# Routing steps, pooling adds and weight splits at other turns, and the gate of the expert output on ScalarE

## The chip, the cores and the metric

The kernel runs on one core of one Trainium2 chip. Its five engines work side by side and meet at semaphores: TensorE (PE in the profile; its weight loads are PEld), VectorE (DVE), ScalarE (ACT), GpSimd (POOL) and SyncE (SP), which here only issues DMAs. The metric is the device time of one execution in microseconds (us), lower is better; of several executions the median is taken.

## The reference

Attention over pooled keys, and behind it a mixture of eight experts of which each row uses one:

```python
# q, k, v: 8 batches x 8 heads x 576 rows x 64
k_p = k.reshape(B, H, 72, 8, D).mean(axis=3)      # 8 rows pooled to one
v_p = v.reshape(B, H, 72, 8, D).mean(axis=3)
scores = scale * q @ k_p.T;  attn = softmax(scores)
x = (attn @ v_p)                                   # as 4608 rows x 512
logits = x @ w_gate                                # 4608 x 8
expert = argmax(logits);  gate_w = softmax(logits)[expert]
# a row's position: how many rows before it chose the same expert;
# rows at positions from capacity (N // E * 2 = 1152) on are dropped
h = relu(x_of_expert @ w1[e])                      # 512 -> 1024
y = h @ w2[e]                                      # 1024 -> 512
out[row] = gate_w[row] * y                         # dropped rows: 0
```

All is float32. The inputs q and k are drawn eight times larger than v, so that the softmax is far from flat.

## The kernel before, in words

**Two parts.** The first (to about 216 us) computes attention, decides for each row its expert and its place among that expert's rows, and writes for each slot of each expert which row it holds and with which gate. The second is a loop over tiles of an expert's rows. In both, instructions are issued in program order on each engine (`manual_schedule`): what the text of the kernel emits first on an engine runs first there, and waits there for whatever it needs while all behind it waits too.

**Turns.** The attention works on 36 units of 128 query rows by four heads. Two batches make a pair, a pair has 9 units (`NPU`), and pair p has units 9p to 9p + 8. The loop `for n in range(nu + 2)` (L1028) has 38 turns, n = 0 to 37. "Turn n" below means that iteration. In it unit n is scored (`score`, L479), its maximum taken and subtracted on VectorE (`softmax`; `mx`, `pt`), the next unit's queries transposed (`pq`, L462) and copied by ScalarE to `qT` (L463), and the exponential taken on ScalarE. Unit n - 2 is finished: its weights are transposed (`p_t`, `pp` L502), copied by ScalarE to `pT` (L503), multiplied by the values (`av`, `pa`, L516), and normalised on VectorE (`norm`: `rz` L527, then `xo` and, last, the gate logits `lt` L542). The next unit's `pa` uses the same PSUM tile, so its first product waits for `lt` of the unit before. The value products and the logits share one product: the gate matrix is multiplied into the values beforehand. `n_early` is 25 and `n_start` 33; in `hooks`, `p, j = divmod(n, 9)`.

**Queues written by hand.** Work that is not a unit's own is kept in lists of functions or generators and pulled in small steps at set places of a turn (`step(queue, n)`):

- `rq`, the routings: nearly all on VectorE. One step in `softmax`, the call at L1078 with a number of steps that depends on the turn, and three steps in `norm`. One `route` (L588 on) covers 9 columns of 128 rows: maximum of the logits `gmx`, difference `gd` (L598), the choice `gme` and `gmm`, the one-hot rows `oh` (L614), their sums `su` (L621), a running count, then three empty steps where more than three columns are routed (L631 to L633), count products on TensorE (`po`, L641, 8 to 32 columns wide), position arithmetic (`gps`, `gpos`, `ghi` L662, `gix`), and the gate's reciprocal into `pairs` (L672). Routing 0 enters the queue in turn 10, routing 1 in turn 19, routing 2 in turn 28; three short ones (routing 3) come in turns 32, 35 and 37.
- `sq`, the scatters of `pairs` into `slots` in DRAM (L679, POOL): nine for each routing, two a turn, four a turn from turn 26. `slots` is first filled with a default by a DMA (`setup_rows`, L339), called in `hooks` where n is 12. For routing 1 each scatter has a copy of `mx` to the tile `apart` ahead of it, so that POOL waits for that turn's maximum.
- `gq`, POOL's pooling adds (three adds to a piece of keys or values, `tree`, L370 on) of the pair after next, four a turn; `hooks` puts them in the queue. From turn 26 on the queue holds instead eight pieces of the favourite expert's w1: each is a ScalarE cast `w1h` (L125) and a POOL subtraction `w1l` (L126).
- `dq`, the masks of the capacity (VectorE, turn 27); `hq` and `aq`, preparation of keys, values and loads.

In turns 31 to 34 rows of the favourite expert are gathered and transposed (`pxe`), and in turns 36 and on the first expert tile is begun (`hidden`, `prologue`).

**The loop over tiles** (`For_i`, L1157 on) makes 20 iterations for the input, 15 on two tiles of 128 rows, 5 on one. All float32 products are made as three products of a rounded part and a remainder (`xh`/`xl`, `w1h`/`w1l`, `hh`/`hl`, `w2h`/`w2l`; ScalarE casts, VectorE subtracts). An iteration reads its numbers from a table into registers on each engine (`values_load`), computes h (`hidden_all`, L150: four groups `g` in turn on three PSUM tiles `ph`; ScalarE's relu `hh` L1129 and VectorE's `hl` L1130 empty each), y (`product`, L159) of tile 1 and of tile 0, and between them transposes the next rows (`px`, L1117). Where the next iteration has another expert (`sw`), `split_w1` and `split_w2` cast and subtract the new weights, which SP has loaded one iteration earlier (`load_w1`, `load_w2` into `r1`, `r2`, L118 and L122; a load may start when the splits of the iteration have read them). Both tiles of y are scaled by their rows' gates (`gate`, L1152, on VectorE: `ys`), and POOL scatters them to the output behind a small subtraction that waits for `ys` (`guardf`), after scattering rows of zeros for the dropped ones (`zrow`).

Of the kernel before, what the change touches and what calls it, by code (L numbers as in the profile page):

```python
# [10 lines left out]
F32 = mybir.dt.float32  # L11
# [20 lines left out]
def pooled_attn_top1_moe(ctx: ExitStack, tc: tile.TileContext, q, k, v, wg, w1, w2, cap, out):  # L32
# [129 lines left out]
    with ExitStack() as actx:  # L162
# [421 lines left out]
        def route(bp, t0, G, blk, tail, prods, sc, count=False, run=None):  # L584
# [45 lines left out]
            if gn > 3:  # L630
                yield  # L631
                yield
                yield  # L633
            po = bank([P, 512], "po")[:, 0 : 4 * E].rearrange("p (a e) -> p a e", a=4)
            prods = [x for x in prods if before or x[1] != "c"]
            for n_, (w, x, l, m) in enumerate(prods):
# [102 lines left out]
        with tc.manual_schedule():  # L739
# [265 lines left out]
            def hooks(n):  # L1005

                p, j = divmod(n, NPU)
                if n == 0:
                    red(vps[0][:, NR - 1 :], raws[0][1][2][:, 2:3])
                    pooled(1)  # L1010
                    pool(1)
                if p == B // 2:
                    return
                if p + 2 < B // 2:
                    if j == (4 if p == 0 else 2):
                        load_kv(p + 2)
                    if j == (7 if p == 0 else 5):
                        if p:
                            nc.gpsimd.tensor_copy(apart, early["mx"][:, 0, 0:1])
                        pooled(p + 2)  # L1020
                        pool(p + 2)
                if n == 3 * NB:
                    drain(gq)
                    gq.append(setup_rest())
                    drain(gq)
                    setup_rows()

            for n in range(nu + 2):  # L1028
                u = units[n] if n < nu else None
                p = units[n - 2] if n > 1 else None  # L1030
                nx = units[n + 1] if n + 1 < nu else None
                new = n and u and u.b != units[n - 1].b
                if new:
                    assert not aq
                    ahead(u.b)
                if n == n_start:
                    start_weights()
                if n == n_early:
                    start_early()
                if n == n_early + 1:  # L1040
                    drain(gq)
                    split_early(0, 2 * KD, nc.gpsimd)
                if n == n_early + 3:
                    start_ids()
                if n == n_early + 4:
                    start_rows()
                if u:
                    u.score(0)
                if p:
                    p.p_t(0)  # L1050
                if u:
                    u.score(1)
                    u.softmax()
                step(aq)
                if p:
                    p.p_t(1)
                if n == nu + 1:
                    for c in range(KF):
                        nc.scalar.copy(wr["h"][:, c], wr[2][:, c])
                if n >= nu:  # L1060
                    hidden(0, n - nu)
                if nx:
                    nx.q_part()
                flush()
                step(aq)
                if n == 1:
                    busy(5)
                    hq.append(prep_v(0))
                    step(hq)
                if u:  # L1070
                    u.exp()
                if p:
                    p.open()
                    p.av(0)
                turns(n)
                if p:
                    p.av(1)
                step(rq, 4 if NPU < n < nu - 8 else 8 if n >= nu - 8 else 0)  # L1078
                step(dq)
                if p:  # L1080
                    p.norm()
                    r = route_of(p)
                    if r:
                        rq.append(r)
                        if p.b == early_b - 1:
                            rq.append(favourite())
                hooks(n)
                step(gq, 4 if n <= n_early else 0 if n_early + 3 <= n < n_early + 5 else 2)
                step(sq, 2 if n < nu - 10 else 4)
                step(aq)  # L1090
            flush()
# [4 lines left out]
    with ExitStack() as bctx:  # L1096
# [52 lines left out]
                split(hh[s], hl[s], p)  # L1149

        def gate(i):
            nc.vector.tensor_scalar_mul(ys[i], y[i], io[:, i, 1:2].bitcast(F32))  # L1152

        nc.sync.dma_start(xs[NT : NT + 1, :], zrow[0:1])
        nt = nc.values_load(ntl[0:1, 0:1], min_val=E, max_val=MT // 2 + E)
# [1 line left out]
        with tc.For_i(0, nt, 1, iteration_sync="reg_based") as t:  # L1157
            with tc.manual_schedule():
                two = nc.values_load(cf[0:1, 5, ds(t, 1)], min_val=0, max_val=1)  # L1159
                sw = nc.values_load(cf[0:1, 0, ds(t, 1)], min_val=0, max_val=1)  # L1160
                nw = nc.values_load(cf[0:1, 1, ds(t, 1)], engines=(SP,), min_val=0, max_val=1)
                we = nc.values_load(cf[0:1, 2, ds(t, 1)], engines=(SP,), min_val=0, max_val=E - 1)
                ct = nc.values_load(cf[0:1, 3, ds(t, 1)], engines=(DVE,), min_val=0, max_val=NCOL)  # L1163
                c2 = nc.values_load(cf[0:1, 3, ds(t + 2, 1)], engines=(DVE,), min_val=0, max_val=NCOL)  # L1164
                cd = nc.values_load(cf[0:1, 4, ds(t, 1)], engines=(DVE,), min_val=0, max_val=NCOL)  # L1165
                nc.gpsimd.tensor_sub(io, zi, zi)
                nc.gpsimd.tensor_sub(iz, zi[:, 0], zi[:, 0])
                with tc.If(two > 0) as both:
                    hidden_all()
                    product(y[1], hh, hl, 1)  # L1170
                    transpose_x()
                    product(y[0], hh, hl, 0)
                with both.Else():
                    hidden_one()
                    product(y[0], hh, hl, 0)
                with tc.If(sw > 0):
                    split_w1(0)
                masked(ix[:, :, 0], c2, mkeep)
                gather(xg, ix, xs[:, :])
                split_x()  # L1180
                with tc.If(sw > 0):
                    split_w1(1)
                load_w1(we, cond=nw > 0, bounds_check="skip_entire_dma")
                columns(io[:, :, 1], ids[:, ds(ct, 2), 1])
                masked(io[:, :, 0], ct, mkeep)
                gate(1)
                masked(iz, cd, mdrop)
                nc.gpsimd.tensor_sub(guard[:, 0], iz, iz)
                for i in range(2):
                    scatter(iz[:, i : i + 1], zrow[:, :], across_iterations=True)  # L1190
                gate(0)
                with tc.If(sw > 0):
                    split_w2()
                load_w2(we, cond=nw > 0, bounds_check="skip_entire_dma")
                for i in (1, 0):
                    nc.gpsimd.tensor_sub(guardf, ys[i][:, 0:2], ys[i][:, 0:2])
                    scatter(io[:, i, 0:1], ys[i][:, :], across_iterations=True)
# [26 lines left out]
```

## Time and profile before

| what | time |
|---|---|
| median of 3 executions | 639.11 us (638.94 to 639.9) |
| the profiled execution | 639.53 us |
| its span, first to last instruction | 637.5 us |
| mean granted TensorE clock | 0.987 of full |

| stretch, us | PE busy | DVE busy | ACT busy | POOL busy | granted clock |
|---|---|---|---|---|---|
| 0 to 216, attention and routing | 206.32 | 156.88 | 114.13 | 137.18 | 0.98 |
| 216 to 628, the loop | 407.75 | 174.87 | 122.20 | 155.78 | 1.00 |
| 628 to 637.5, last scatters | 0.00 | 0.75 | 0.00 | 4.41 | 0.66 |

In the lines of the profile below an arrow `out<-in` names the tiles written and read; L598 is a line of the kernel; a group's "x40 | 30.0, 751" is its count, total us and mean ns; a timeline row begins with its start and its duration in us, and "[2.13 <-DVE lt L542]" is the time its engine stood idle before it and what ended that. A row of windows gives the stretch, its length, each engine's busy us with its number of instructions (PE, PEld, DVE, ACT, POOL), the granted clock, and the DMA share and rate.

### The profile page before, as it was taken

To read this page: it belongs to the slowest core of one execution; us is meant where nothing else is said; L and a number is where in the kernel's file an instruction comes from. 1 tells how busy PE (TensorE), PEld (TensorE's weight loads), DVE (VectorE), ACT (ScalarE), POOL (GpSimd) and SP (SyncE) were. 2 spreads that over 40 slices of the span, in tenths; PEclk is the share of its full clock that TensorE was granted. 3 is DMA by queue.
4 is the path that set the end of the run, shared out by engine and by line. 5 is a ranking of instruction groups with operands and counts; after the bars stand their busy time and mean duration, and the time that the engine had idled before them with its cause. 6 is when DMAs were issued, how large, how long until landed. Compare 5 with 4: busy or idle time off the path is not lost.

```text
span 637.5 us, 14824 instructions
## 1 busy us (share of the span) xinstructions
PE 614.1 (96%) x4249; PEld 554.1 (87%) x4250; DVE 332.5 (52%) x720; ACT 236.3 (37%) x403; POOL 297.4 (47%) x468
## 2 busy tenths in 40 slices
PE   9899999899999999999899999999999999999994
PEld 8889899798889889988789989988899888989983
DVE  4667868777788322268447731326422585323222
ACT  2555576366544211157245511117111472111111
POOL 7799499253743422424435522434434145441344
PEclk9999999799999999999999999999999999999997
DMA  9989953283191610228728640213612181210112
GB/s 325 359 330 323 349 183 122 72 258 101 53 329 53 230 35 33 66 81 309 241 82 308 230 141 33 66 33 120 235 47 66 41 282 36 66 51 19 62 49 66
DMA packets 47084, 93.81 MB, mean 147 GB/s; under 512 B 13392, under 2 KB 23632, under 8 KB 47060
## 3 DMA queue, kind: packets, MB, share of 16 engines
q1 hardware_dynamic: 30836, 60.37, 27.6%
q0 software_dynamic: 11392, 21.57, 11.3%
q10 hardware_dynamic: 4832, 11.56, 4.8%
q8 instruction: 14, 0.23, 0.1%
q14 instruction: 10, 0.08, 0.0%
HBM read 132.97 MB, written 31.27 MB: 258 GB/s over the span
## 4 chain that ended last, share of the span: by engine, by line
PE 60%; DVEq 2%; issue 2%; DVE 1%; POOL 1%; ACT 0%; POOLq 0%; ACTq 0%
PE y L159 30%; PE ph L150 23%; PE ph L1140 4%; PE px L1117 2%; PE ph L1147 1%; DVE w2l L126 0%; POOL out_dram L100 0%; DVE hl L1130 0%; DVEq L1165 0%; DVEq L1164 0%; DVEq L1163 0%; ACT w2h L125 0%; DVEq L1160 0%; DVEq L1159 0%; POOL xg L95 0%
## 5 line engine op out<-in xcount | busy, mean ns | idle before, releaser
L1129 ACT ACTIVATE hh<-ph 128x512 fp32r<-128x512 f32 x60 | 35.8, 598 | 170.1 <-PE ph L150 170.0
L1130 DVE SCALAR_TENSOR_TENSOR hl<-ph,hh 128x512 fp32r<-128x512 f32 x60 | 40.7, 690 | 109.4 <-ACT hh L1129 62.5
L150 PE MATMUL ph<-xh,w1h 128*128 128x256 f32 x480 | 76.5, 282 | 4.6 <-DVE hl L1130 3.9
L150 PE MATMUL ph<-xh,w1l 128*128 128x256 f32 x480 | 75.9, 281 | 0.0
L150 PE MATMUL ph<-xl,w1h 128*128 128x256 f32 x480 | 75.9, 281 | 0.0
L150 PEld LDWEIGHTS ph<-xh,w1h 128*128 128x128 f32 x480 | 65.8, 189 | 6.9 <-DVE hl L1130 4.8
L159 PE MATMUL y<-w2h,hh 128*128 128x512 f32 x280 | 71.7, 398 | 0.0
L95 POOL DMA_INDIRECT xg<-xs,ix x42 | 43.5, 1035 | 58.2 <-PE y L159 50.0
L516 PE MATMUL pa<-vbd,pT 96*128 96x146 f32 (+1 forms) x480 | 67.1, 296 | 3.5 <-DVE lt L542 3.5
L159 PE MATMUL y<-w2h,hl 128*128 128x512 f32 x280 | 69.3, 390 | 0.0
L159 PE MATMUL y<-w2l,hh 128*128 128x512 f32 x280 | 69.2, 389 | 0.0
L150 PEld LDWEIGHTS ph<-xl,w1h 128*128 128x128 f32 x480 | 65.2, 190 | 0.0
L150 PEld LDWEIGHTS ph<-xh,w1l 128*128 128x128 f32 x480 | 64.7, 189 | 0.0
L516 PEld LDWEIGHTS pa<-vbd,pT 96*128 96x128 f32 (+1 forms) x480 | 57.1, 181 | 6.8 <-DVE lt L542 4.5
L159 PEld LDWEIGHTS y<-w2l,hh 128*128 128x128 f32 x280 | 52.6, 188 | 11.1
L159 PEld LDWEIGHTS y<-w2h,hl 128*128 128x128 f32 x280 | 52.6, 188 | 10.9
L100 POOL DMA_INDIRECT out_dram<-zrow,iz x40 | 51.3, 1282 | 16.9 <-issue 14.9
L159 PEld LDWEIGHTS y<-w2h,hh 128*128 128x128 f32 x280 | 49.6, 188 | 9.6 <-ACT hh L125 0.9
L126 DVE TENSOR_TENSOR xl<-px,xh 128x512 fp32r<-128x512 f32 x40 | 25.8, 686 | 60.9 <-ACT xh L125 60.9
L93 POOL TENSOR_TENSOR guard<-ix 128x2 int32<-128x2 int32 x21 | 4.0, 193 | 101.5 <-DVE ix L90 96.8
L503 ACT COPY pT<-pp 96x384 f32<-96x384 f32 x72 | 33.8, 474 | 45.0 <-PE pp L502 44.4
L679 POOL DMA_INDIRECT slots<-pairs,gix x36 | 35.4, 983 | 30.3 <-DVE pairs L672 13.0
(236 smaller groups left out, 1051.8 us busy)
## 6 DMA issues: line engine op xcount, KB each, us to landing
r<-in_moe_w_dram SPq DMA_DIRECT2D x84, 1024.0 KB, 11.1
raw<-in_k_dram SPq DMA_DIRECT2D x12, 768.0 KB, 6.5
raw<-in_v_dram SPq DMA_DIRECT2D x12, 768.0 KB, 10.6
xs<-xo ACTq DMA_DIRECT2D x16, 512.0 KB, 3.1
qblk<-in_q_dram SPq DMA_DIRECT2D x14, 512.0 KB, 7.7
raw<-in_moe_w_dram SPq DMA_DIRECT2D x4, 512.0 KB, 4.8
r<-in_moe_w_dram ACTq DMA_DIRECT2D x2, 1024.0 KB, 6.9
qblk<-in_q_dram SPq DMA_DIRECT2D x4, 256.0 KB, 8.3
```

What stands on the lines that cost most here:

```text
L95: nc.gpsimd.indirect_dma_start(out=dst[:, i, :].bitcast(F32), out_offset=None, in_=src, in_offset=bass.IndirectOffsetOnAxis(ap=ix[:, i, 0: ...
L100: ins = nc.gpsimd.indirect_dma_start(out=out[:, :], out_offset=bass.IndirectOffsetOnAxis(ap=i_, axis=0), in_=src, in_offset=None, bounds_c ...
L126: eng.tensor_sub(lo, src, hi.bitcast(F32))
L150: nc.tensor.matmul(p[:, f2], a[:, c, f * P : (f + 1) * P], b[:, c], start=(f2 == 0 and j == 0 and c == 0), stop=(f2 == 1 and j == 2 and c ...
L159: nc.tensor.matmul(y, a[:, c, i * P : (i + 1) * P], b[:, c], start=(n == 0), stop=(n == 3 * KF - 1))
L503: nc.scalar.copy(self.pT[:, j], pp[0:KC, 0:HC])
L516: nc.tensor.matmul(self.pa[us, j, h0 * XW : (h0 + 2) * XW], self.pT[:, j, c, us], vbd[b % 2][:, cc].rearrange("r a x -> r (a x)"), start=( ...
L679: ins = nc.gpsimd.indirect_dma_start(out=slots[:, :], out_offset=bass.IndirectOffsetOnAxis(ap=ix[:, g, 0:1], axis=0), in_=pairs[:, pr + g0 ...
L1117: nc.tensor.transpose(px[i][:, c], xg[:, i, c * P : (c + 1) * P], identr)
L1129: nc.scalar.activation(hh[s], p, AF.Relu)
L1130: nc.vector.scalar_tensor_tensor(out=hl[s], in0=p, scalar=0.0, in1=hh[s].bitcast(F32), op0=ALU.max, op1=ALU.subtract)
L1140: nc.tensor.matmul(ph[f], a[:, c, r], b[:, c, fs], start=(j == 0 and c == 0), stop=(j == 2 and c == KD - 1))
```

## The change

It has five edits.

1. `route`: one more empty step ahead of the count products, in the routings of more than three columns (0, 1 and 2, and the first of routing 3).
2. `rq`: eight steps at L1078 instead of none up to turn 9 and four up to turn 13; four from turn 14 as before, eight in the last as before.
3. `hooks`: the pooling adds of pair 3 enter their queue in turn 13 (j = 4) instead of 14; pair 2's stay in turn 7, and the copy of `mx` to `apart` stands in turn 12, ahead of `setup_rows`, instead of ahead of the adds.
4. `gq` from turn 26: two pieces of w1 in turn 26, then one at the end of each turn and, in turns 27 and 28, one more ahead of and one more behind the second scores. Before, it was two a turn at the ends, with none in turns 28 and 29.
5. The loop: `gate` is a ScalarE activation (copy with a scale for each row) instead of a VectorE multiplication, and both gates, tile 1 first, stand behind `split_w2`.

```diff
@@ route
                 yield
                 yield
                 yield
+                yield
             po = bank([P, 512], "po")[:, 0 : 4 * E].rearrange("p (a e) -> p a e", a=4)
@@ hooks
-                    if j == (7 if p == 0 else 5):
-                        if p:
-                            nc.gpsimd.tensor_copy(apart, early["mx"][:, 0, 0:1])
+                    if j == (7 if p == 0 else 4):
                         pooled(p + 2)
                         pool(p + 2)
                 if n == 3 * NB:
                     drain(gq)
                     gq.append(setup_rest())
                     drain(gq)
+                    nc.gpsimd.tensor_copy(apart, early["mx"][:, 0, 0:1])
                     setup_rows()
@@ for n in range(nu + 2)
+                more = 1 if n_early + 1 < n < n_early + 4 else 0
                 if u:
                     u.score(0)
                 if p:
                     p.p_t(0)
+                step(gq, more)
                 if u:
                     u.score(1)
                     u.softmax()
                 step(aq)
                 if p:
                     p.p_t(1)
+                step(gq, more)
...
-                step(rq, 4 if NPU < n < nu - 8 else 8 if n >= nu - 8 else 0)
+                step(rq, 8 if n < 2 * NPU - 4 or n >= nu - 8 else 4)
...
-                step(gq, 4 if n <= n_early else 0 if n_early + 3 <= n < n_early + 5 else 2)
+                step(gq, 4 if n <= n_early else 2 if n == n_early + 1 else 1)
@@ gate, and the loop
         def gate(i):
-            nc.vector.tensor_scalar_mul(ys[i], y[i], io[:, i, 1:2].bitcast(F32))
+            nc.scalar.activation(ys[i], y[i], AF.Copy, scale=io[:, i, 1:2].bitcast(F32))
...
                 masked(io[:, :, 0], ct, mkeep)
-                gate(1)
                 masked(iz, cd, mdrop)
                 nc.gpsimd.tensor_sub(guard[:, 0], iz, iz)
                 for i in range(2):
                     scatter(iz[:, i : i + 1], zrow[:, :], across_iterations=True)
-                gate(0)
                 with tc.If(sw > 0):
                     split_w2()
+                for i in (1, 0):
+                    gate(i)
                 load_w2(we, cond=nw > 0, bounds_check="skip_entire_dma")
```

## The prediction

> **What bounds the kernel now.** I read the page first, then TensorE's rows in the view of waits, then the windows.
>
> ```profile
> span 637.5 us, 14824 instructions
> PE 614.1 (96%) x4249; PEld 554.1 (87%) x4250; DVE 332.5 (52%) x720; ACT 236.3 (37%) x403; POOL 297.4 (47%) x468
> ...
> PE ph L150 <- DVE hl L1130: 3.9, 4, 1.8
> PE pa L516 <- DVE lt L542: 3.5, 4, 2.1
> PE po L641 <- DVE su L621: 1.9, 2, 1.2
> ```
>
> TensorE is busy for 614.1 of 637.5 us, so only its gaps can be won. The three largest waits (total, times, longest) are on VectorE: 3.9 us in the loop over tiles (L150), 3.5 us where a unit's attention product waits for the last unit's `lt` (L516), 1.9 us where a routing's count products wait for `su` (L641). That is 9.3 us, but busy time is not all useful: the clock column says more.
>
> ```profile
> 112.21:115.62 3.41, 2.28 (x19) 2.06 (x20) 2.81 (x7) 0.52 (x1) 0.07 (x1) 1.00 0.21 72
> 115.62:119.03 3.41, 3.41 (x18) 3.39 (x20) 1.39 (x6) 0.32 (x2) 0.00 (x0) 0.50 0.00 0
> 119.03:122.45 3.42, 3.42 (x23) 2.27 (x20) 2.44 (x12) 0.47 (x1) 0.00 (x0) 0.50 0.00 0
> ...
> 153.17:156.58 3.41, 2.70 (x24) 2.50 (x24) 3.24 (x13) 1.55 (x4) 0.00 (x0) 1.00 0.57 214
> 156.58:159.99 3.41, 3.41 (x17) 3.30 (x17) 1.70 (x6) 0.95 (x2) 0.00 (x0) 0.50 0.02 7
> 177.06:180.48 3.42, 2.23 (x22) 1.94 (x19) 2.99 (x14) 1.06 (x3) 1.94 (x4) 1.00 0.87 258
> ...
> 216.00:628.00 412.00, 407.75 (x2600) 366.36 (x2600) 174.87 (x285) 122.20 (x177) 155.78 (x237) 1.00 0.34 113
> ```
>
> Each row is a stretch, its length, the busy time of PE, PEld, DVE, ACT and POOL, then the granted clock. I cut the stretches where the clock changes: 115.62 to 122.45 and 156.58 to 159.99 are at 0.50, and those lengths and their distance are multiples of 3.41 us. At half clock, 3.41 us do 1.71 us of work: the first closing cost 3.4 us, the second 1.7. Ahead of each lies a window with a wait and little dense work (2.28 and 2.70 busy; in the second the busy part holds the routing's products of 8 to 32 columns). But 177.06 to 180.48, with 2.23 busy, was not followed by a closing: busy time alone does not decide. So two waits of turns 20 and 29 cost 5.1 us of clock besides themselves. In the loop TensorE is busy for 407.75 of 412 us at full clock.
>
> **The change part by part.** *Routing 1 (turns 20 and 21; earlier pooling).*
>
> ```profile
> 107.83 1.59 DVE L598 TENSOR_TENSOR gd<-lg,gmx 128x72 f32<-128x72 f32 x1
> 109.98 1.69 DVE L614 TENSOR_TENSOR oh<-cw,gmm 128x64 fp32r<-128x64 f32 x1
> ...
> 107.51 1.81 POOL L370 TENSOR_TENSOR t<-raw 128x768 f32<-128x768 f32 x1
> 110.57 1.01 POOL L372 TENSOR_TENSOR t<-t 128x384 f32<-128x384 f32 x1
> ...
> 113.06 0.22 DVE L542 TENSOR_TENSOR lt<-pa,rz 128x64 f32<-128x64 f32 x1
> 113.34 1.01 PE L516 MATMUL pa<-vbd,pT 96*128 96x146 f32 x6 [2.13 <-DVE lt L542]
> ```
>
> Two small VectorE operations took 1.59 and 1.69 us. Each ends within 0.1 us of a pooling add on POOL (109.32 and 111.58), so they stood behind those adds. `lt` came late, and TensorE waited 2.13 us. The change queues these adds one turn earlier (j 5 to 4). Does POOL run them earlier?
>
> ```profile
> 69.50 0.23 DVE L614 TENSOR_TENSOR oh<-cw,gmm 128x64 fp32r<-128x64 f32 x1
> 71.39 1.02 PE L516 MATMUL pa<-vbd,pT 96*128 96x146 f32 x6 [0.41 <-DVE lt L542]
> 79.98 1.17 POOL L679 DMA_INDIRECT slots<-pairs,gix x1 [9.01 <-DVE rz L527]
> ...
> L339 SPq DMA_DIRECT2D slots<-ids x1: 434/434/434, 66.9 to 66.9; - x1
> DMA to landing us min/median/max: 12.2/12.2/12.2
> ```
>
> In POOL's order the adds stand behind routing 0's first two scatters. Those also move one turn earlier, so the order stays: two scatters, four adds, two scatters. The first scatter must follow the landing of `slots<-ids`, which it overwrites: 66.9 + 12.2 = 79.1. It ran at 79.98, so at most 0.9 us can be won, and the copy of `mx` that stood ahead of the adds (0.2 us, estimate from the 0.22 of `lt`, no smaller) is gone. I take -0.15 (0 to -1.1): the collision stays. The moved copy waits for turn 12's maximum while POOL has nothing else that could run.
>
> *Routing 0 (8 steps a call until turn 13).* `su` and the running count now come ahead of turn 11's norm: from the 69.50 row on, some 0.5 us more VectorE work before `lt`. The products move from the end of turn 12 to between turn 12's scores and its second transposes. There TensorE waits some 0.4 us for `su`, which takes the place of the 0.41 in the row of 71.39. The last eight small operations (about 0.2 us each, partly overlapped: 1.3 us) now stand ahead of turn 12's norm. TensorE has some 0.8 us to spare there, so turn 13 starts 0.45 us late (estimate; 0 to 1.3). This is absorbed: turn 20's wait ends when POOL's adds let VectorE go, whenever TensorE arrives. If that collision were gone, the 0.45 would stay. The extra step does nothing in turns 20 and 21: routing 1's products stay in the same call.
>
> *Routing 2 (one empty step more; the earlier w1 split).*
>
> ```profile
> 153.49 0.22 DVE L598 TENSOR_TENSOR gd<-lg,gmx 128x72 f32<-128x72 f32 x1
> 154.28 0.23 DVE L614 TENSOR_TENSOR oh<-cw,gmm 128x64 fp32r<-128x64 f32 x1
> 155.28 0.28 PE L641 MATMUL po<-su,matr 128*128 128x16 f32 x1 [0.71 <-DVE su L621]
> ...
> 161.88 2.49 POOL L126 TENSOR_TENSOR w1l<-raw,w1h 128x512 fp32r<-128x512 f32 x2 [9.83 <-ACT w1h L125]
> 163.32 1.11 DVE L662 TENSOR_SCALAR ghi<-gpos 128x9 f32<-128x9 f32 x1
> 166.34 1.01 PE L516 MATMUL pa<-vbd,pT 96*128 96x146 f32 x6 [0.75 <-DVE lt L542]
> ```
>
> Counted out, the products were the 12th step, the last norm step of turn 29; as the 13th they fall behind turn 30's maximum. TensorE then has turn 30's scores and first transposes to do while VectorE finishes `su`: -0.71. Without the idle stretch right beside the tiny products I expect no half-clock window: -1.71. Late next is turn 30's subtraction, behind the counts, but its exponential is used two turns later.
>
> All eight pieces of w1 are split by turn 28 instead of 31. So POOL's subtraction at 161.88, behind which `ghi` stood for 1.11 us, is gone from turn 30; of the 0.75 at 166.34 I leave 0.3, since VectorE has the last six steps ahead of that norm: -0.45 (0 to -0.75).
>
> ```profile
> 145.98 1.12 ACT L125 CAST w1h<-raw 128x512 fp32r<-128x512 f32 x2
> 147.53 0.66 PE L462 MATMUL pq<-identr,qblk 128*128 128x128 f32 x4 [0.28 <-ACT pT L503]
> ...
> 151.24 0.47 ACT L503 COPY pT<-pp 96x384 f32<-96x384 f32 x1
> 151.80 0.62 PE L462 MATMUL pq<-identr,qblk 128*128 128x128 f32 x4
> ```
>
> The price lies on ScalarE, 0.56 us a cast. In turn 27 two of three casts move into the turn: the 0.28 wait goes, and 0.05 for a later `qT` comes. The eighth cast now stands at the end of turn 28, ahead of the copy at 151.24, which then ends at 151.24 + 0.56 + 0.47 = 152.27. TensorE's `pq` would be ready at 151.80 - 0.27 = 151.53: a new wait of 0.75 (0 to 1.3).
>
> *The loop: gates on ScalarE behind the casts of w2.*
>
> ```profile
> L1152 DVE TENSOR_SCALAR ys<-y,io 128x512 f32<-128x512 f32 x40 | 30.0, 751 | 30.2 <-PE y L159 30.2
> L965 ACT ACTIVATE xo<-ps,idp 128x512 f32<-128x512 f32 x1 | 0.7, 690 | 4.9 <-PE ps L159 4.9
> ...
> 239.11 0.75 DVE L1152 TENSOR_SCALAR ys<-y,io 128x512 f32<-128x512 f32 x1 [2.38 <-PE y L159]
> 244.19 0.69 DVE L1130 SCALAR_TENSOR_TENSOR hl<-ph,hh 128x512 fp32r<-128x512 f32 x1 [4.33 <-issue]
> ...
> 300.68 2.00 ACT L125 CAST w2h<-r 128x1024 fp32r<-128x1024 f32 x2 [1.43 <-DMA r<-in_moe_w_dram]
> 301.45 4.62 DVE L126 TENSOR_TENSOR w2l<-r,w2h 128x1024 fp32r<-128x1024 f32 x4
> 307.81 0.74 PE L150 MATMUL ph<-xh,w1h 128*128 128x256 f32 x4 [1.84 <-DVE hl L1130]
> ```
>
> VectorE loses 40 x 0.751 = 30 us, ScalarE gains 40 x 0.69 = 28. Most of that was free: in a plain iteration the gate waits for `y` (239.11), then VectorE's queue reads its registers for 4.33 us, and even `hl` at 244.19 made nobody wait. Behind ScalarE's gate now stand its register reads and the next relu. Had they to wait as long as VectorE's, relu and `hl` would come where `hl` came before: no cost. What counts are the four waits of 3.9 us, after one-tile iterations that switch weights. There VectorE's register reads follow the last subtraction, which waits for the last cast of w2. The cast stays ahead of the gates, so it moves only where it waited for the load of w2 (300.68). That load is released by the subtractions of the iteration before, which now start up to 0.8 us earlier. Two waits can gain, each 0 to 0.8; I take -0.7 together (0 to -1.5).
>
> At the end POOL's scatters come last; the gate's time is hidden behind the zero-row scatters either way.
>
> Sum: -0.15 - 0.71 - 1.71 - 0.45 - 0.28 + 0.05 + 0.75 - 0.7 = -3.2 us. The profiled execution took 639.53 us (2.0 around its span), so it would give 636.3; against the median of 639.11 it is **636.0**, rounded up.
>
> The clock of these rows can be set against a rule. The Trainium skill, page TensorE: Matmul & The Clock Gate (Part 1: The HAM clock gate), has the clock halve after an idle window of about 3.4 us. The trace agrees on the 3.41 us, not on idle: windows with 2.28 and 2.70 us busy were followed by half clock. By the rule as written no wait here would close the gate, and the sum without its clock term would be -1.5.
>
> **The rivals.** *The gate stays open in turn 21 too.* The window that closed it held 2.28 us busy; with the wait 0.15 us shorter at its end and 0.45 at its start, or the grid elsewhere, it may no longer be too thin. 177.06 (2.23 busy, not followed by a closing) speaks for it, the unmoved adds against. One open window more is -1.7, both -3.4: 634.3 to 632.6, taken as 632.9. Four executions within 1 us (638.94 to 639.9) speak for a grid fixed to the kernel's start. The same section of the Trainium skill calls the windows free-running; no run here shows that, and by it the chance of this rival would be drawn anew in each execution.
>
> *It does less than it says.* The idle time moves instead of going: the new wait of 0.75 at turn 29, or the product gap in turn 12, makes a thin window elsewhere (+1.7), or `su` is as late as before (+0.7). 637.0 to 639.2, taken as 637.9.
>
> *Slower.* POOL's w1 subtractions (1.25 us each) now fill about 143 to 153 us, across the masks of turn 27 and the start of routing 2. If two VectorE operations stand behind them as `gd` and `oh` did, the product of turn 28 waits some 2.5 us, and if that closes the gate for two windows, 3.4 more: +5.9 - 3.2 gives 641.8. It decides from a wait of about 2 us there. Against it: two blocked operations need adds back to back, and most of VectorE's work there reads PSUM, as `lt` and `xo` do, which no add delayed.
>
> **How the numbers follow.** Forecast 636.0: 0.42. Open gate, 632.9: 0.33. Less than it says, 637.9: 0.15, of which 0.10 lies within 0.2% of 639.11 (637.8 to 640.4, about what a measurement of this kernel can tell from no change) and 0.05 below. Slower, 641.8: 0.10. Faster is 0.42 + 0.33 + 0.05 = 0.80, same 0.10, slower 0.10. The range runs from 632.0, below both open windows, to 638.8, which leaves out the slower case, a few hundredths of the third and a little below.
>
> **What would show it.** Right: no L641 wait in turn 29 and clock 1.00 there; `ghi` near 0.17 to 0.33 us in turn 30; a new `pq` wait of 0.5 to 1 us in turn 29; `gd` and `oh` of turn 20 still over 1 us; gates of 0.69 us on ScalarE, L150's waits at 2.5 to 3.9 us. Wrong: POOL's first slots scatter well before 79 us, a clock of 1.00 from 115 to 123 us, any half clock outside turns 21 and 22, or new waits of L516 in turns 27 to 29.

## The result, and the profile after

The changed kernel is slower: a median of 645.4 us (642.05 to 648.25, 7 runs) against 639.22 us for the kernel before beside it, a ratio of 1.0126 with a 95% interval of 1.0083 to 1.017. The forecast was 636.0, the range 632.0 to 638.8. The ratio and its interval, here and among the experiments, are taken over the single executions without the slow ones, and so are not the quotient of the two medians. The profiled execution of the changed kernel took 644.84 us, its span is 643.1.

The page's head, and then TensorE's rows in the view of waits (total, times, longest), of the changed kernel:

```profile
span 643.1 us, 14922 instructions
PE 618.9 (96%) x4249; PEld 557.2 (87%) x4250; DVE 307.5 (48%) x680; ACT 261.9 (41%) x443; POOL 300.6 (47%) x468
...
PE pa L516 <- DVE lt L542: 5.7, 3, 5.3
PE ph L150 <- DVE hl L1133: 1.4, 4, 0.4
PE pq L462 <- PE pp L502: 1.3, 2, 0.9
PE po L642 <- DVE su L621: 1.2, 1, 1.2
```

The waits that the change was to shorten did shrink: `hl` in the loop from 3.9 to 1.4 us, `su` from 1.9 to 1.2. But `lt` now has one wait of 5.3 us that was not there, and `pq` one of 0.9. TensorE's busy time rose by 4.8 us (614.1 to 618.9) though it does the same 4249 matmuls: that is half clock. The windows that carry it, on this execution's grid of 3.41 us (columns as in the prediction: stretch, length, busy time of PE, PEld, DVE, ACT and POOL, clock):

```profile
69.20:72.61 3.41, 2.23 (x19) 1.82 (x18) 3.34 (x10) 1.11 (x3) 1.26 (x11) 1.00 0.98 331
72.61:76.02 3.41, 3.41 (x19) 3.13 (x18) 0.15 (x1) 1.17 (x2) 0.00 (x0) 0.50 1.02 423
76.02:79.44 3.42, 3.42 (x18) 2.60 (x18) 2.74 (x13) 0.00 (x0) 0.00 (x0) 0.50 0.98 339
79.44:82.85 3.41, 3.41 (x19) 2.63 (x20) 2.38 (x5) 0.95 (x2) 2.93 (x4) 0.50 0.42 140
...
116.98:120.40 3.42, 3.42 (x33) 3.17 (x33) 1.93 (x4) 1.28 (x3) 0.00 (x0) 1.00 0.37 131
120.40:123.81 3.41, 3.41 (x22) 2.26 (x22) 2.24 (x12) 0.47 (x1) 0.00 (x0) 0.50 0.00 0
...
147.70:151.12 3.42, 1.56 (x14) 1.27 (x12) 3.42 (x1) 2.75 (x6) 3.42 (x4) 1.00 0.10 26
151.12:154.53 3.41, 0.00 (x0) 0.00 (x0) 3.34 (x9) 0.00 (x0) 1.79 (x2) 1.00 0.00 0
154.53:157.94 3.41, 3.33 (x14) 2.88 (x15) 1.45 (x3) 1.41 (x3) 0.00 (x0) 0.50 0.00 0
157.94:161.36 3.42, 3.42 (x17) 3.33 (x16) 1.58 (x5) 2.04 (x5) 1.58 (x3) 0.50 0.00 0
```

Six windows at 0.50 instead of three: three from turn 12 on, one in turn 21, two from turn 28 on, 6 x 1.71 = 10.2 us instead of 5.1. In the window from 151.12 to 154.53 TensorE does nothing at all.

To see where the time was lost and won, read when each turn starts: the start of VectorE's maximum `mx`, after less before. Each change in this difference is the gain or loss of one turn.

| turn | before, us | after, us | difference | what lies between |
|---|---|---|---|---|
| 12 | 71.52 | 71.14 | -0.38 | start of the kernel |
| 14 | 80.69 | 85.93 | +5.24 | +5.6: three half-clock windows and a wait in turn 12 |
| 20 | 106.31 | 111.55 | +5.24 | nothing |
| 23 | 125.86 | 127.41 | +1.55 | -3.7: no wait in turn 20, one half-clock window less |
| 27 | 143.74 | 145.29 | +1.55 | nothing |
| 29 | 151.97 | 161.52 | +9.55 | +8.0: the wait of 5.3 us and its half clock |
| 31 | 166.62 | 173.71 | +7.09 | -2.5: the turns of routing 2, without the half clock they had before |
| 35 | 184.25 | 191.34 | +7.09 | nothing |
| end of the span | 637.5 | 643.1 | +5.6 | -1.5: the loop |

**The wait of 5.3 us.** The timeline of the changed kernel in turns 27 and 28, start and duration first:

```profile
146.75 6.17 POOL L126 TENSOR_TENSOR w1l<-raw,w1h 128x512 fp32r<-128x512 f32 x5
146.81 0.14 DVE L344 CAST capf<-capt 128x1 f32<-128x1 int32 x1
...
146.99 6.10 DVE L346 TENSOR_SCALAR mkeep<-spos,capf 128x288 int32<-128x288 f32 x1
...
153.02 0.36 DVE L346 TENSOR_SCALAR mdrop<-spos,capf 128x288 int32<-128x288 f32 x1
...
154.61 0.61 PE L516 MATMUL pa<-vbd,pT 96*128 96x146 f32 x1 [5.34 <-DVE lt L542]
```

The first mask operation, `mkeep`, took 6.10 us. Its twin `mdrop`, of the same size, took 0.36. POOL ran five subtractions of w1 without a gap from 146.75 to 152.92, and `mkeep` ended 0.2 us after the last. Behind it on VectorE stood the norm that ends in `lt`, and for `lt` TensorE waited.

**Turn 12.** The same view, around routing 0's count products:

```profile
69.95 0.25 PE L642 MATMUL po<-su,matr 128*128 128x16 f32 x1 [0.24 <-ACT ex L654]
...
71.14 0.75 DVE L486 TENSOR_REDUCE mx<-ps 128x8 f32<-128x576 f32 x1
...
71.94 0.16 DVE L647 SCALAR_TENSOR_TENSOR gps<-po,oh 128x8 f32<-128x8 f32 x1
...
72.19 0.69 PE L462 MATMUL pq<-identr,qtail 128*128 128x128 f32 x4 [0.94 <-PE pp L502]
```

The products `po` take one of the two PSUM banks in turn; `pq` is the next to want that bank, and it is free when VectorE has read `po` into `gps`, which stands behind `mx`. The row names `pp`, which was long done; `gps` ended at 72.10, and `pq` started at 72.19. So TensorE waits 0.94 us, in a stretch filled with products of 8 to 32 columns.

### The profile page after: what moved, and what is told of

Same layout as the page of the kernel before. It is cut to its first block, busy times and chain, and to the rows that moved or that the text cites. A ratio compares the mean times of both kernels' runs of the same rounds, so it can differ in the third digit from the quotient of the medians.

```text
span 643.1 us, 14922 instructions
## 1 busy us (share of the span) xinstructions
PE 618.9 (96%) x4249; PEld 557.2 (87%) x4250; DVE 307.5 (48%) x680; ACT 261.9 (41%) x443; POOL 300.6 (47%) x468
## 5 line engine op out<-in xcount | busy, mean ns | idle before, releaser
L516 PE MATMUL pa<-vbd,pT 96*128 96x146 f32 (+1 forms) x480 | 69.4, 302 | 5.8 <-DVE lt L542 5.7
L516 PEld LDWEIGHTS pa<-vbd,pT 96*128 96x128 f32 (+1 forms) x480 | 59.2, 186 | 9.2 <-DVE lt L542 6.8
```

The lines of the kernel that those rows point to most:

```text
L516: nc.tensor.matmul(self.pa[us, j, h0 * XW : (h0 + 2) * XW], self.pT[:, j, c, us], vbd[b % 2][:, cc].rearrange("r a x -> r (a x)"), start=( ...
```

## The experiments

Each kernel ran beside the kernel before on one chip; the ratio is to that kernel's runs in the same job. The turn differences are against the profile of before, as in the table above.

| run | what it is | median, us | before beside it | ratio, 95% interval |
|---|---|---|---|---|
| e1 | after, w1 split as before | 636.84 | 637.53 | 0.9977 (0.9951 to 1.0004) |
| e2 | after, masks in turn 24 | 636.36 | 637.53 | 0.9984 (0.9954 to 1.0013) |
| e3 | after, routing rate as before | 638.85 | 637.53 | 1.0025 (1.0000 to 1.0049) |
| e4 | before, gates moved | 637.69 | 637.53 | 1.0014 (0.9984 to 1.0044) |
| e5 | before, one empty step | 636.24 | 638.81 | 0.9987 (0.9947 to 1.0027) |
| e6 | before, pooling moved | 633.29 | 638.81 | 0.9910 (0.9888 to 0.9933) |
| e7 | after, masks in turn 24, old rate | 629.79 | 638.81 | 0.9858 (0.9819 to 0.9897) |
| e8 | after, old rate, old w1 split | 630.46 | 638.97 | 0.9875 (0.9836 to 0.9914) |
| e9 | after, gaps between subtractions | 639.33 | 638.81 | 1.0045 (1.0003 to 1.0087) |
| e10 | e2, filler in routing 0's bank | 634.94 | 638.97 | 0.9947 (0.9915 to 0.9980) |
| e11 | e2, filler in `pa` | 636.47 | 637.96 | 0.9971 (0.9935 to 1.0006) |

**The w1 split put back (e1) and the masks moved (e2).** Two ways to take the suspected collision of turn 27 apart, one from POOL's side and one from VectorE's.

```diff
 e1: after.py
-                more = 1 if n_early + 1 < n < n_early + 4 else 0
+                more = 0
-                step(gq, 4 if n <= n_early else 2 if n == n_early + 1 else 1)
+                step(gq, 4 if n <= n_early else 0 if n_early + 3 <= n < n_early + 5 else 2)
```

> The changed kernel with the w1 split put back to the turns it had before (two pieces a turn, none in turns 28 and 29). Theory: in turn 27 the mask operation on VectorE stood 6.1 us behind five POOL subtractions without a gap, TensorE waited 5.3 us for it, and the idle stretch closed the clock for two windows (3.4 us). Without them: mkeep back to about 0.4 us, no long L516 wait in turn 28, 645.4 - 5.3 - 3.4 + 0.5 (ghi behind a subtraction in turn 30 again) = 637, between 634 and 640 since the clock's windows may lie elsewhere. Rival, the wait comes from turn 12's delay or from the casts on ScalarE: 643 to 646.

```diff
 e2: after.py
-                if b == LAST - 1:
-                    dq.append(masks)
...
+                if n == n_early - 1:
+                    dq.append(masks)
                 if n == n_early:
                     start_early()
```

> The changed kernel with the masks computed in turn 24 instead of 27, where POOL subtracts nothing; the w1 split stays early. Theory (masks behind the subtractions): both mask operations at 0.4 us, no wait over 1 us in turns 27 to 29, 645.4 - 8.7 = 636.7, between 633.5 and 639. Rival, another VectorE operation of turn 27 or 28 then stands behind the five subtractions, or the six casts on ScalarE hold up the transposes: a wait of 1 to 4 us remains there, 640 to 645.

Both came out as the theory had them: 636.84 and 636.36. The rows of the tile `mkeep` in e2 (duration in ns, then first and last start):

```profile
L346 DVE TENSOR_SCALAR mkeep<-spos,capf x1: 370/370/370, 132.2 to 132.2; 128x288 int32<-128x288 f32 x1
```

From turn 27 to 29 the difference to before moved by 8.0 us in the changed kernel, by -0.02 in e1 and -0.5 in e2. So it takes both, the subtractions and the masks, to make the wait, and with either elsewhere it is gone. In e2 turn 31 comes 0.7 us earlier than in e1 (-2.32 against -1.62): that is what the early split was worth together with the masks out of the way; no run parts the two.

e2 shows besides what the subtractions did not hold up. Rows of POOL and VectorE from its turns 26 to 28:

```profile
141.57 2.51 POOL L126 TENSOR_TENSOR w1l<-raw,w1h 128x512 fp32r<-128x512 f32 x2 [3.27 <-ACT w1h L125]
...
143.59 0.39 DVE L556 TENSOR_REDUCE lg<-lt 128x16 f32<-128x128 f32 x1
...
145.37 6.19 POOL L126 TENSOR_TENSOR w1l<-raw,w1h 128x512 fp32r<-128x512 f32 x5
...
146.01 0.20 DVE L527 RECIPROCAL rz<-rz 128x8 f32<-128x8 f32 x1
...
147.20 0.76 DVE L486 TENSOR_REDUCE mx<-ps 128x8 f32<-128x576 f32 x1
```

The reduction `lg` and the reciprocal `rz` read and write SBUF alone, and took 0.39 and 0.20 us beside subtractions, as they do elsewhere (medians of 0.38 and 0.20 in the kernel before). So not every operation on SBUF is held: `mkeep`, a TENSOR_SCALAR, was; this reduction and this reciprocal were not.

**The old rate of the routing steps (e3).**

```diff
 e3: after.py
-                step(rq, 8 if n < 2 * NPU - 4 or n >= nu - 8 else 4)
+                step(rq, 4 if NPU < n < nu - 8 else 8 if n >= nu - 8 else 0)
```

> The changed kernel with the old number of routing steps a call, so that routing 0's count products stay at the end of turn 12. Theory: in turn 12 the products take a bank that is not free before VectorE has added them, behind the maximum, and the next transposes wait 0.94 us; the thin window (2.23 of 3.41 us busy) closed the clock for three windows. Without it: clock 1.00 from 65 to 90 us and 645.4 - 0.6 - 5.1 = 639.7, between 638 and 643, since turn 20 may get its old wait back. Rival, the phase of the clock's windows alone decides and the place of the products does not matter: half clock in turn 12 again, about 645.

Turn 12's loss went (difference at turn 14: -0.14), and the median is 638.85. What the expectation had not: turn 20's wait did not come back either (difference at turn 22: -5.20). The masks' collision of course stayed, POOL's and VectorE's rows again:

```profile
139.51 6.17 POOL L126 TENSOR_TENSOR w1l<-raw,w1h 128x512 fp32r<-128x512 f32 x5
...
139.75 6.11 DVE L346 TENSOR_SCALAR mkeep<-spos,capf 128x288 int32<-128x288 f32 x1
```

**The gates alone (e4).** The loop's edit of the change, put into the kernel before.

```diff
 e4: before.py
-            nc.vector.tensor_scalar_mul(ys[i], y[i], io[:, i, 1:2].bitcast(F32))
+            nc.scalar.activation(ys[i], y[i], AF.Copy, scale=io[:, i, 1:2].bitcast(F32))
...
-                gate(1)
...
-                gate(0)
                 with tc.If(sw > 0):
                     split_w2()
+                for i in (1, 0):
+                    gate(i)
```

> The kernel before with the loop's edit alone: gates on ScalarE behind the casts of w2. Theory: the four waits for hl after an expert switch fall from 3.9 us in total to 1.4, as in the changed kernel, and nothing else changes: 639.2 - 2 = 637.2, between 636.2 and 638.2. Rival, the waits only move to ScalarE (relu behind the gate and the register reads): 638.8 to 640.

```profile
PE ph L150 <- DVE hl L1130: 2.3, 4, 1.0
```

The waits for `hl` fell to 2.3 us in its profile, not to the expected 1.4; the medians can't tell it from the kernel before. The profiles of all runs say more: from turn 35's `mx` to the end of the span it is 451.1 to 452.0 us in the ten profiles with the gates on ScalarE (mean 451.5), and 453.3, 452.0 and 452.0 in the three without (before, e5, e6). The means differ by about 0.9 us, but e4's own 452.0 is that of e5 and e6, so the gain may be anything from nothing to about that. Part of the kernel before's 3.9 us of waits was that execution's own: e5 and e6, with the old gates, have 2.7 and 2.6 us of them, and e7, with the new ones, 2.8.

**The empty step alone (e5), and the pooling adds alone (e6).**

```diff
 e5: before.py
                 yield
                 yield
                 yield
+                yield
             po = bank([P, 512], "po")[:, 0 : 4 * E].rearrange("p (a e) -> p a e", a=4)
```

> The kernel before with one empty step more ahead of the count products. Theory (the prediction's term for routing 2): its products leave the end of turn 29, the 0.7 us wait for su there goes, turn 31 starts some 0.7 us earlier, and where the clock closed in turn 29 another 1.7 us: about 1 to 2 us under the kernel before of the same job, routings 0 and 1 unchanged. Rival, su or the bank makes TensorE wait in turn 30 as long as before in turn 29: no difference.

```diff
 e6: before.py
-                    if j == (7 if p == 0 else 5):
-                        if p:
-                            nc.gpsimd.tensor_copy(apart, early["mx"][:, 0, 0:1])
+                    if j == (7 if p == 0 else 4):
...
                     drain(gq)
+                    nc.gpsimd.tensor_copy(apart, early["mx"][:, 0, 0:1])
                     setup_rows()
```

> The kernel before with the third edit alone: pair 3's adds queued in turn 13, the routing at its old number of steps. Theory: the scatters of routing 0 still come in the turn they had, so the first four adds run ahead of them, in POOL's idle time from 72 to 77 us, and POOL's last add ends near 106 instead of 112 us; gd and oh of turn 20 fall back to 0.23 us, the 2.1 us wait goes and with it the clock's closing there: 2 us less at turn 21 and up to 5.5 us in an execution whose clock closed there: 632 to 635, the spread of the kernel before smaller. Rival (the prediction's reasoning, that the first scatter's landing holds the adds): adds end within 1 us of before, no difference.

By its ratio e5 can't be told from the kernel before, so only its profile says something. There the turns 29 to 31 gain 1.74 us, the half-clock window. The wait itself was not won: one of the same kind as in turn 12 took its place, this time in turn 30. TensorE's row:

```profile
158.40 0.63 PE L462 MATMUL pq<-identr,qtail 128*128 128x128 f32 x4 [0.59 <-PE pp L502]
```

Is the open clock the step's doing? e6 has the old steps. Its TensorE row in turn 29, and two windows (its own grid is not known, since its clock never changed):

```profile
150.36 0.28 PE L641 MATMUL po<-su,matr 128*128 128x16 f32 x1 [0.71 <-DVE su L621]
...
148.41:151.82 3.41, 2.70 (x24) 2.50 (x23) 3.24 (x14) 1.55 (x4) 0.00 (x0) 1.00 0.57 216
151.82:155.24 3.42, 3.42 (x33) 3.22 (x31) 1.74 (x5) 2.36 (x5) 0.00 (x0) 1.00 0.01 5
```

TensorE waited 0.71 us for `su` as in the kernel before, and no half clock followed; turns 29 to 31 gain 1.56 us without the step. So the wait does not close the clock each time. Of the three profiles without the step, before and e4 have half clock between turns 29 and 31 and e6 has none; e1, e2, e5 and e7 to e11, all with the step, have none either (in the changed kernel and e3 the masks had closed it just ahead). That speaks for the step, but one profile of each can't give its worth.

e6 is the surprise: one edit of the five, and 0.9% faster than the kernel before, with runs between 631.49 and 635.41 where the kernel before ran between 631.54 and 640.53. POOL's and VectorE's rows of e6:

```profile
72.01 1.81 POOL L370 TENSOR_TENSOR t<-raw 128x768 f32<-128x768 f32 x1
...
105.62 0.59 POOL L374 TENSOR_TENSOR vp<-t 128x192 f32<-128x192 f32 x1
...
108.46 0.23 DVE L598 TENSOR_TENSOR gd<-lg,gmx 128x72 f32<-128x72 f32 x1
...
109.25 0.23 DVE L614 TENSOR_TENSOR oh<-cw,gmm 128x64 fp32r<-128x64 f32 x1
```

With the old rate, routing 0's scatters enter POOL's queue in the turn they had, so the adds stand ahead of them and run from 72 us on, while the scatters wait for `slots` to land. The last add ends at 106.21 instead of 112.28, and `gd` and `oh` take 0.23 us instead of 1.59 and 1.69.

**Both causes taken away (e7), and the smaller version (e8).** e7 is e2's and e3's edits together; e8 is e1's and e3's together.

> The changed kernel with the masks in turn 24 and the old number of routing steps: both causes of the loss taken away, the rest of the change kept. Theory: e3's profile less the wait of 5.4 us and less the closing of 5.1 us there, 637.2 - 10.5 = 626.7; a closing elsewhere adds 1.7 each: 626 to 631, below every run of the kernel before. Rival, the two fixes hit each other as turn 12's delay and turn 20's collision did (arriving earlier, TensorE meets another collision): 632 to 637.

> The changed kernel with edits 2 and 4 undone (old number of routing steps, old w1 split, masks in turn 27): the empty step, the shifted pooling adds and the gates on ScalarE are left. Theory: no collision in turn 12, 20, or 27; ghi stands behind a subtraction in turn 30 again, which cost 0.7 us between e1 and e2: e7's 629.8 + 0.7 = 630.5, between 629 and 632. Rival, the early split of w1 is worth more or less than that: under 629.5 or over 632.

Both beat the kernel before clearly, e7 by 1.4% and with all six runs between 628.81 and 630.58. Its waits:

```profile
PE ph L150 <- DVE hl L1133: 2.8, 4, 1.2
PE ps L479 <- ACT qT L463: 1.2, 2, 0.7
PE po L642 <- DVE su L621: 1.2, 1, 1.2
...
PE pq L462 <- ACT pT L503: 0.6, 1, 0.6
PE pp L502 <- DVE vbd L442: 0.6, 1, 0.6
PE pa L516 <- DVE lt L542: 0.6, 3, 0.2
```

No wait for `lt` is over 0.2 us, and no window of its profile before the end of TensorE's work is at half clock. e7's median lies 3 us above the 626.7 of its expectation, which had added e3's half clock in full to its wait of 5.4 us: half clock that falls into a wait costs nothing, and from turn 27 to 29 e3 had lost 8.0 us, not 10.5. e8 came out where it was expected, 0.7 us behind e7.

**Gaps between the subtractions (e9).** What holds VectorE, one POOL instruction or a row of them?

```diff
 e9: after.py
+            def spaced(*a):
+                split(*a)
+                for _ in range(2):
+                    nc.gpsimd.memset(apart, 0.0)
...
-                    gq.append(partial(split, w1h[:, c, fs], w1l[:, c, fs], early["w1"][c][:, fs], eng))
+                    gq.append(partial(spaced, w1h[:, c, fs], w1l[:, c, fs], early["w1"][c][:, fs], eng))
```

> The changed kernel with two tiny POOL memsets behind each subtraction of w1, the masks left in turn 27. Theory A, VectorE gets in at the first end of a POOL instruction that has another kind of instruction behind it (as gd and oh did in the kernel before): mkeep takes at most 1.7 us instead of 6.1, the wait of 5.3 us falls below 1.5 us, about 637 to 640. Theory B, VectorE is held as long as POOL has work in its queue: mkeep over 6 us, wait over 5 us, about 645. Either way the subtractions end up to 2 us later.

The timeline of e9, turn 20 and turn 27:

```profile
110.57 1.69 DVE L614 TENSOR_TENSOR oh<-cw,gmm 128x64 fp32r<-128x64 f32 x1
...
145.96 2.03 DVE L346 TENSOR_SCALAR mkeep<-spos,capf 128x288 int32<-128x288 f32 x1
...
146.51 1.28 POOL L126 TENSOR_TENSOR w1l<-raw,w1h 128x512 fp32r<-128x512 f32 x1
...
147.72 0.31 POOL L827 MEMSET apart<- 128x1 f32 x2
```

`mkeep` now ended 0.2 us after the first subtraction beside it (147.79), at the memsets, instead of after the fifth. It is a little over the 1.7 us of theory A, since it had begun during the scatter ahead; theory B is out. But its twin was then held by the second subtraction (147.93 to 149.20):

```profile
147.92 1.48 DVE L346 TENSOR_SCALAR mdrop<-spos,capf 128x288 int32<-128x288 f32 x1
```

So TensorE still waited 2.40 us for `lt`, where theory A had under 1.5. The ratio of e9 to the kernel before is 1.0045, the changed kernel's 1.0126. Six of its twelve executions, this one among them, took under 638 us, and six 640.7 to 644.7; what differed in those is not known. In this profile turn 12 kept its clock (difference at turn 14: +1.04), and TensorE met the collision of turn 20 again: `oh` took 1.69 us. In the changed kernel the delay of turn 12 had hidden it; POOL's last add and `oh` of that profile:

```profile
111.14 0.59 POOL L374 TENSOR_TENSOR vp<-t 128x192 f32<-128x192 f32 x1
...
114.23 0.23 DVE L614 TENSOR_TENSOR oh<-cw,gmm 128x64 fp32r<-128x64 f32 x1
```

**Filling turn 12 (e10, e11).** Four matmuls on zeros, whose results are overwritten or not read, were to keep TensorE at work there.

```diff
 e10: e2's kernel
-            po = bank([P, 512], "po")[:, 0 : 4 * E].rearrange("p (a e) -> p a e", a=4)
+            early["z"] = bank([P, 512], "po")
+            po = early["z"][:, 0 : 4 * E].rearrange("p (a e) -> p a e", a=4)
...
+                if n == 3 * NB:
+                    busy(4, early["z"][:, 256:])
                 if n == nu + 1:
```

> e2 (masks in turn 24) with four idle 128-column matmuls on TensorE, 0.275 us each, in turn 12 between the second transposes and the wait for the bank of routing 0's products. Theory: the gate closed there because that stretch held little dense work, so with the gap filled it stays open (clock 1.00 from 65 to 100 us) and turn 14 starts 4 us earlier; TensorE then reaches turn 20 while POOL still adds, oh takes over 1 us again, TensorE waits about 2 us and the gate may close there: the gain is given back, 634 to 638, no clear difference to e2's mean of 635.9. Rival, the closing of turn 12 comes from something else (the products themselves, the phase): half clock from about 72 us as in e2's profile.

```diff
 e11: e2's kernel
+                if n == 3 * NB:
+                    p.open()
+                    busy(4, p.pa[:, 0])
                 if n == nu + 1:
...
-                    p.open()
+                    if n != 3 * NB:
+                        p.open()
                     p.av(0)
```

> e2 with the same four idle matmuls of turn 12 written to the unit's own pa tile, which is free once lt of turn 11 is done, so that they stand in the gap and not behind the wait for the bank as e10's did. Theory (little dense work closes the gate): clock 1.00 from 65 to 100 us in the profile, turn 14 within 1.5 us of the kernel before; TensorE then meets POOL's adds in turn 20 (oh over 1 us, a wait of about 2 us, perhaps a closing there). The time would change little, 632 to 638. Rival, the gap does not matter and the tiny products or the phase close the gate: half clock from about 72 us again, turn 14 over 4 us late.

Neither settles it. In e10 the filler stood behind the same wait for the bank (0.9 us for `gps`) and the clock closed from 73.3 to 83.6 us all the same. In e11 it ran in the gap, the clock stayed at 1.00 and turn 14 was +1.35 late; but e9, with no filler, had stayed open too, and both had the grid of windows at the same place (to 0.02 us). So e11 does not separate filler from grid. Both times lie within the expectation.

## Why the prediction was wrong

- **The w1 split: the step that failed.** The prediction had "The price lies on ScalarE, 0.56 us a cast" and -0.45 on POOL's side. The price lay on VectorE behind POOL: a wait of 5.3 us and two windows of half clock, both gone in e1 and e2. It stood among the rivals as "Slower", with the right place (the masks of turn 27) and the right two windows, but with a wait of 2.5 us and a chance of 0.10. The terms of this part add up to +0.07 us, and turns 27 to 29 lost 8.0. The size was off because `gd` and `oh` had each been held by one add, and I took that as the price of one blocked operation. Behind `gd`'s add came a memset, and e9 shows that memsets let VectorE in; behind `oh`'s came an add that depends on it, and that this does the same was not tried. (`oh` had also begun 0.6 us ahead of its add, during a scatter.) Five subtractions whose casts were all done left no gap, and one operation stood for all of them. "Most of VectorE's work there reads PSUM" was true and of no help: one that does not was enough. The terms on ScalarE were fair: `pq`'s new wait was 0.6 us in e7, for 0.75.
- **Routing 0: the size failed, and "This is absorbed" held by luck.** The delay at full clock was 1.2 us (e9, turns 12 to 14) for 0.45, the missing part being the wait for the bank; and the rival's product gap, put at one window, closed three in the profiles of the changed kernel, e1, e2 and e10. In e1 and e2 the delay of 5.4 us at turn 20 was down to 0.2 at turn 23: TensorE came too late for the collision of turn 20 and was spared its wait and its two windows. The prediction had a small delay swallowed by a collision that stays; in these profiles a loss as large took the collision's place.
- **Routing 1 and the pooling: right, for an order that was read right and not followed up.** POOL's last add ended 0.55 us earlier, within the bound, and between 0.9 us earlier (e1) and 0.9 later (e10) in the other profiles with both edits; the collision of turn 20 stayed where TensorE was on time (`oh` 1.69 us in e9, 1.68 in e11). That it was gone from the changed kernel's profile, -3.7 us, is the 5.2 us by which TensorE came late. The prediction saw that the two edits cancel ("so the order stays") and did not ask what either gives alone: e6 gains 0.9%.
- **Routing 2:** -1.71 for the clock fits e5 (-1.74 in all), but e6 gained 1.56 there without the step, so its worth is not shown. The 0.71 of wait came back as 0.59 at the bank with the old w1 split (e1, e5, 0.60 in e8), and did not with the early one and no collision (e2, e7).
- **`ghi`:** -0.45 forecast, of a wait of 0.75. No `ghi` of the changed kernel took over 0.17 us, as forecast, and the wait for `lt`, 0.81 us in e1, is gone from e2. The two differ by 0.7 us in all, with the masks' place and the bank's wait in it.
- **The loop:** -0.7 forecast, -1.5 in the profile of the change, about -0.9 by the means of all profiles, nothing by e4 against e5 and e6.
- **The clock:** "Four executions within 1 us speak for a grid fixed to the kernel's start" was wrong. The grids of the two profiles differ: half clock begins at 115.62 in the one, at 120.40 in the other, 1.40 windows of 3.41 us apart. The kernel before alone ran between 631.54 and 640.53 us in the job of e5, with mean granted clocks of 0.996 and 0.985 in these two executions. The Trainium skill, page TensorE: Matmul & The Clock Gate (Part 1: The HAM clock gate), calls the windows free-running; these traces agree.

## What to carry to other kernels

Before moving POOL work beside VectorE work, list the VectorE operations of that stretch that read only SBUF and are of a kind that a profile shows held (here two-tensor and tensor-scalar operations), and price each at the whole uninterrupted row of POOL instructions ahead, not at one. When two edits are found to cancel in a queue's order, price each of them alone: here one alone (e6) was 0.9% faster than the kernel before, and all with two parts put back (e8) 1.25%. And where several small products take a bank from a rotation of two, ask when the engine that reads them will do so; the next user of that bank waits for it.

## What the runs showed of the hardware

- Some VectorE operations on SBUF alone wait through POOL additions or subtractions that follow each other without a gap: `mkeep` took 6.10 us beside five, 2.03 beside the end of a scatter and one, and its twin 0.36 once POOL had stopped. Others do not: `lg` and `rz` took their usual 0.39 and 0.20 us beside the subtractions of e2, and `mx`, which reads PSUM, took 0.76 there (0.74 to 0.76 in all turns of the kernel before). What a scatter does is open: the `mkeep` of e2, begun 0.1 us into one, took 0.37 us, and that of e9, begun 0.5 us into one, did not end before the subtraction behind it had. The Trainium skill, page SBUF — State Buffer (SBUF: two separate sides), has VectorE, in some kinds of operation, and GpSimd share a port pair, held "for the whole instruction" by whichever starts first. The trace agrees that one is blocked; by that sentence `mkeep` would have been free after one subtraction of 1.25 us, and the measurement says after the fifth.
- What closes the clock is not settled. A window with 1.56 us busy (147.70) was not followed by a closing, the empty one after it (151.12) was, and so was one with all 3.42 busy (116.98, with eight small products); afterwards it stayed at half for one, two or three windows, though TensorE was busy throughout (before, changed kernel). And a wait of 0.71 us in turn 29 came with a closing in the kernel before and with none in e6. Neither busy time nor the filler explains it.
